# Loading the first units of a fused attention and MLP kernel over three DMA queues, and a new order of loads on a fourth engine's queue

## The chip, the cores and the metric

The kernel runs on one core of a Trainium2 chip. A core has a matrix engine (TensorE, PE; its weight loads are shown apart as PEld), a vector engine (VectorE, DVE), a scalar engine (ScalarE, ACT), GpSimd (POOL) and SyncE (SP), each with its own in-order queue of instructions, and 16 DMA engines that serve all of them. SP and ACT issue transfers over hardware queues; GpSimd issues them over a software queue, whose transfers can also turn fp32 into bf16 on the way. The metric is the device time in microseconds (us), the median of several runs; less is better.

## The reference

A retention layer (attention with decay in place of softmax) feeds a two-layer MLP with exact GELU.

```python
def _attn_ref(q, k, v):                       # each (8, 8, 576, 64) fp32: batch, heads, positions, head size
    scores = scale * np.matmul(q, k.transpose(0, 1, 3, 2))
    gamma = 1.0 - 2.0 ** (-5.0 - np.arange(H, dtype=np.float32))
    rel = pos[:, None] - pos[None, :]
    Dmat = np.where(rel >= 0, gamma[:, None, None] ** rel[None, :, :], 0.0)
    return np.matmul(scores * Dmat[None, :, :, :], v)

x = attn_out.transpose(0, 2, 1, 3).reshape(4608, 512)
h = x @ w_in                                  # (512, 2048)
g = 0.5 * h * (1.0 + erf(h / sqrt(2)))
out = g @ w_out                               # (2048, 512)
```

## The kernel before

**Units.** The 576 positions of each of the 8 batches are cut into chunks of 128 with a tail of 64. A unit is one chunk of one batch (or two tails together); 36 units of 128 rows give the 4608 rows of x. Four units are one block of 512 rows of the MLP. Units 0 to 3 are the first chunks of batches 0 to 3 and need nothing from earlier chunks; they stand alone, later units go in pairs.

**A unit's path.** q and k are turned by PE (`turn`, line 401, into PSUM tile qk_ps, copied by DVE or ACT into qkT), multiplied into scores (`scores`, line 439, tile sc), multiplied on DVE by the decay mask (`masked`, line 488, tile ret, line 507; for first chunks the mask is near, made by ACT at line 164), and multiplied by v on PE (`inner`, line 523, tile o_ps). DVE also makes vh, v scaled by the decay (line 516), from which `state` (line 548, tile u_ps) builds what later chunks need. `evacuate` (line 622) copies o_ps into x; later chunks are multiplied there by dqT (line 636). dqT is extended by four products on GpSimd (line 280), the items dq2, dq3, dq4 and dq0 of the load order. Then follow the first MLP product (`mlp1`, line 652, tile hT, Gelu on ACT into g_all) and the second (`mlp2`, line 683, tile oT, for block 0; a seven-product scheme, `mlp2_fast`, for the others, whose operands wt are four pairs of subtractions of w_out, line 715).

**The planner.** All instructions are put out by a Python loop (line 1110 on) that keeps an estimated time for each engine and chooses PE's next piece of work. It decides with estimated landing times (`land`) and durations; the result is a fixed order on each engine. On the chip the order stays, and semaphores make each instruction wait for its operands. Where nothing is due in the first 16 us, it puts in matmuls on zeros (`warm`, line 1077).

**Loads.** The list ORDER (line 321) is the order of GpSimd's items: wi0 to wi7 and wo0 to wo7 are the eighths of w_in and w_out, q4 the q of unit 4, io the constants, dq a product on dqT. GpSimd keeps up to eight loads in flight: each further one waits for the eighth ahead of it. All loads of units 0 to 3 but two go into the bf16 tile early by this queue. The two are q and k of unit 0: SP and ACT load them as fp32 (line 114), and `either` (line 371) casts them on DVE or ACT, whichever is free first by the planner's count, once `cast_due` (lines 320 and 1049) says that they have landed. A cast is an instruction in that engine's queue, and holds what stands behind it until its load has landed. Line 1146 lets a unit be turned only when its casts are out.

Of the kernel before, what the change touches and what calls it, by code (L numbers as in the profile page):

```python
# [9 lines left out]
FP32 = mybir.dt.float32  # L10
# [7 lines left out]
def kernel(  # L18
# [14 lines left out]
    nc = tc.nc  # L33
    ctx.enter_context(tc.manual_schedule())

    B, H, S, D = q.shape
# [5 lines left out]
    C = 128  # L42
# [28 lines left out]
    N_QKT = 4  # L71
# [4 lines left out]
    ALLOW = 0  # L76
    AHEAD = 14
    RATE = 3.8
    HOT = 7.5
    SLACK, SB, PER_G, PER_B, TURN0 = 1.6, 9.0, 8.0, 40.0, 3.0  # L80
    FINE = 0.38
# [9 lines left out]
    tr_pool = ctx.enter_context(tc.tile_pool(name="tr", bufs=1))  # L91
# [19 lines left out]
    first = {}  # L111
    for nm, src, eng in (("q32", q, nc.sync), ("k32", k, nc.scalar)):
        t = first[nm] = o_pool.tile([128, H, D], FP32, tag="o_sb", name=nm)
        eng.dma_start(t, src[0, :, 0:C, :].rearrange("h s d -> s h d"))
    zeros = ld_pool.tile([128, 512], BF16, tag="v32", bufs=N_V32, name="zeros")
    nc.vector.memset(zeros, 0.0)
    lgh = const.tile([128, H, 1], FP32, name="lgh")
# [34 lines left out]
    def early_slice(n, m):  # L152
        return early[:, n * H * D:(n + m) * H * D]
# [55 lines left out]
            on(engine, dur)  # L209


    sw = [0.0]
    turned = [0.0]
    flying = []
    dq_done = {1}
    land = {}
    loaded = {}
# [11 lines left out]
    def qk_tile(name):  # L229
        return ld_pool.tile([128, 4 * H * D], BF16, tag="qk", bufs=N_LD, name=name)  # L230
# [4 lines left out]
    def tiles_of(i):  # L235
        g = groups[group_of[i]]
        if i not in loaded:
            if i < 4:
                loaded[i] = (early_slice(2 * i, 2).rearrange("p (a h d) -> p a h d", a=2, h=H),
                             early_slice(8 + i, 1).rearrange("p (h d) -> p h d", h=H), None)  # L240
            else:
                n = group_of[i]
                if i != g[0]:
                    qk, kn = loaded[i - 1][0], loaded[i - 1][2]
                elif n not in BY_DVE:
                    qk = qk_tile("qk_ld").rearrange("p (a h j d) -> p a h j d", a=2, h=H, j=2)
                    kn = qk[:, 1]
                else:
                    qk = qk_tile("qkb_ld").rearrange("p (a f) -> p a f", a=2)
                    kn = ld_pool.tile([128, H, 2, D], BF16, tag="kn", bufs=N_KN, name="kn_ld") if len(g) > 1 else None  # L250
                loaded[i] = (qk, None if group_of[i] in BY_DVE else ld_pool.tile([128, H, D], BF16, tag="v", bufs=8, name="v_ld"), kn)
        return loaded[i]
# [12 lines left out]
    def load(what, i):  # L265
# [43 lines left out]
        for jj in (j,) if j is not None else range(2):  # L309
# [3 lines left out]
            else:  # L313
# [2 lines left out]
            land[what, i] = sw_dma(0.88, 0.9) if j is not None else sw_dma(0.68, 0.5)  # L316

    tiles_of(0)
    land["q", 0], land["k", 0] = 4.65, 5.2
    cast_due = {("q", 0): (loaded[0][0][:, 0], first["q32"]), ("k", 0): (loaded[0][0][:, 1], first["k32"])}  # L320
    ORDER = ("wi0 io v0 k1 q1 v1 wi1 q2 k2 v2 wi2 k3 q3 v3 wi3 wi4 wi5 wi6 wi7 wo0 wo1 wo2 wo3 wo4 wo5 wo6 wo7 "
             "q4 k4 q5 k5 v4 v5 dq2 q6 k6 q7 k7 v6 v7 q8 k8 q9 k9 v8 v9 dq3 q10 k10 v10 dq4 q11 k11 q12 k12 n11 n12 dq0").split()

    def next_order():
        item = ORDER.pop(0)
        what = item.rstrip("0123456789")
        load(what, int(item[len(what):] or 0))
# [5 lines left out]
    def reload():  # L333
        if next_load[0] < N_G:
            g = groups[next_load[0]]
            if next_load[0] not in BY_DVE:
                ORDER.extend(f"{what}{i}" for what in "qkv" for i in g)
            else:
                ORDER.extend([f"{what}{i}" for what in "qk" for i in g] + [f"n{i}" for i in g if len(g) > 1])
            next_load[0] += 1  # L340
# [10 lines left out]
    def free_time(n):  # L351
        got = frees(n)
        return free_at[got[-1]] if len(got) == n else 1e9

    def bank(shape, dtype, name):
        b = frees(1)[0]
        held.add(b)
        return b, ps.tile(shape, dtype, tag=b, name=name)

    def release(b, when):  # L360
        held.remove(b)
        free_at[b] = when

    def pe(dur, to="full"):
        if mode[0] != to:
            T["pe"] += 0.11
            mode[0] = to
        T["pe"] += dur * (2.0 if T["pe"] < HOT else 1.0)
        return T["pe"] + DRAIN
# [673 lines left out]
    def fire():  # L1043
        now = T["pe"]
        while ORDER and T["pool"] <= now + 1.5:
            next_order()
# [30 lines left out]
    def warm(n):  # L1077
        b, t = bank([128, 512], FP32, "warm")
        for _ in range(n):
            nc.tensor.matmul(t, lhsT=zeros[:, :128], rhs=zeros, start=True, stop=True)  # L1080
        pe((0.32 if T["pe"] < HOT else 0.2158) * n)
        release(b, T["pe"])
# [22 lines left out]
    for _ in range(N_WARM):  # L1105
        b, t = bank([128, 512], FP32, "warm")
# [3 lines left out]
    while True:  # L1110
# [27 lines left out]
        if nA < N_U:  # L1138
            n = group_of[nA]
            g = groups[n]  # L1140
            if n < nT and nA - nB <= 2 and T["dve"] <= now + SB and g[-1] // 4 <= tM1 + N_XB - 1 and nA + len(g) <= AHEAD + RATE * b1:
                acts.append((max(sg[n]["T"], free_time(2 * len(g))), "S"))
# [53 lines left out]
        gap = min(waits) - now  # L1196
        if now < 16 and gap > (0.6 if now < HOT else 0.2):
            warm(int(gap / 0.6) if now < HOT else max(1, round(gap / 0.23)))
        T["pe"] = max(T["pe"], min(waits))
# [33 lines left out]
```

## Time and profile before

| what | value |
|---|---|
| median of 3 runs | 300.47 us (300.14 to 300.9) |
| profiled execution | 300.81 us, span 298.9 us |
| PE, DVE, POOL, ACT busy | 286.1, 226.7, 152.9, 135.1 us |
| PE: the 15 warm matmuls of line 1080 and 7 of line 1107 | between 1.19 and 14.6 us |
| DMA moved | 34.79 MB, mean 116 GB/s |
| GpSimd's queue, SP's queue, ACT's queue | 17.71, 16.26, 0.26 MB |
| loads of early by GpSimd | 10 of 128 KB, issue to landing 4.9 to 6.1 us |
| w_in, w_out by GpSimd | 8 of 256 KB each, median 7.1 and 9.8 us to landing |

A line of the order of time has the start in us, the time from its first to its last instruction, the engine, the line of the kernel, what is written and read with its shape, the count, and in brackets the idle time of the engine ahead of it with what ended it. A table by stretch has a row for each stretch of time, with each engine's busy time and, at the end, the granted PE clock, the busy share of the 16 DMA engines (transfers overlap, so it can be over 1) and the rate. A DMA queue's line has its packets, megabytes and share of the engines' time.

### The profile page before, as it was taken

What the parts mean: (1) busy time and instruction counts of PE and PEld (TensorE: products, weight loads), DVE (VectorE), ACT (ScalarE), POOL (GpSimd) and SP (SyncE); (2) the same over time, 40 slices, a digit from 0 to 9 for tenths busy, and PEclk for the clock granted to TensorE, in tenths of its full rate; (3) what the DMA queues carried; (4) which work ended last, traced back from release to release, by engine and by line L of the source; (5) the groups of instructions that cost most, each with busy time, mean ns of one, the idle gap of its engine ahead of it and who ended that gap; (6) DMA issues with size and microseconds to landing.
All of it is one profiled execution on the core that took longest, in us unless ns stands there. A gap on an engine that the chain in (4) does not pass through costs nothing.

```text
span 298.9 us, 8793 instructions
## 1 busy us (share of the span) xinstructions
PE 286.1 (96%) x3689; PEld 213.8 (72%) x3718; DVE 226.7 (76%) x432; ACT 135.1 (45%) x262; POOL 152.9 (51%) x232
## 2 busy tenths in 40 slices
PE   7899997999999999999998999999999999999994
PEld 2478555888657656667665666666888888888883
DVE  5762059999999889317969489756998999898751
ACT  7656225744343343542542434433554554546421
POOL 8976797899896899996986842000000000000000
PEclk9999999999999999999999999999999999999998
DMA  9999999999999999999979570201001101111014
GB/s 143 166 186 204 182 187 179 214 163 113 155 141 197 189 201 125 155 162 159 139 126 174 83 188 2 72 2 37 35 2 72 71 2 70 44 28 72 35 55 124
DMA packets 112119, 34.79 MB, mean 116 GB/s; under 512 B 89808, under 2 KB 107728, under 8 KB 112080
## 3 DMA queue, kind: packets, MB, share of 16 engines
q0 software_dynamic: 78048, 17.71, 66.8%
q1 hardware_dynamic: 32992, 16.26, 20.2%
q8 instruction: 29, 0.48, 0.7%
q10 hardware_dynamic: 1040, 0.26, 0.4%
q14 instruction: 10, 0.08, 0.1%
HBM read 42.47 MB, written 9.44 MB: 174 GB/s over the span
## 4 chain that ended last, share of the span: by engine, by line
PE 62%; DMA 16%; POOL 16%; issue 3%; DVE 1%; ACT 0%; POOLq 0%; DVEq 0%; ACTq 0%
PE fa L760 17%; PE hT L656 14%; PE fb L760 13%; PE ha L865 7%; PE hb L865 5%; POOL qkb_ld L298 5%; DMA qkb_ld<-in_q_dram 3%; DMA qk_ld<-in_q_dram 3%; POOL kn_ld L305 3%; DMA kn_ld<-in_k_dram 3%; DMA w_out<-in_moe_w_out_dram 3%; POOL early L315 3%; DMA qk_ld<-in_k_dram 3%; PE sc L462 2%; POOL w_in L270 2%
## 5 line engine op out<-in xcount | busy, mean ns | idle before, releaser
L656 PE MATMUL hT<-x,w_in 128*128 128x512 bf16 (+2 forms) x521 | 92.6, 314 | 3.1 <-DVE x L636 1.0
L656 PEld LDWEIGHTS <-w_in 128*128 128x128 bf16 x544 | 49.1, 98 | 26.1 <-issue 3.2
L661 ACT ACTIVATE g_all<-hT 128x512 bf16<-128x512 f32 x64 | 38.2, 597 | 49.8 <-PE hT L656 47.6
L760 PEld LDWEIGHTS <-g_all 128*128 128x128 bf16 x512 | 49.6, 98 | 11.0 <-issue 0.2
L760 PEld LDWEIGHTS <-s 128*128 128x128 bf16 x384 | 37.4, 98 | 8.9 <-issue 0.2
L746 DVE TENSOR_TENSOR o_sb<-fb,t 128x256 f32<-128x256 f32 x48 | 19.9, 417 | 25.4 <-ACT t L375 12.9
L870 ACT ACTIVATE g_all<-tt 128x512 bf16<-128x512 f32 x36 | 22.6, 630 | 29.4 <-DVE tt L878 29.3
L298 POOL DMA_DIRECT2D qkb_ld<-in_k_dram x56 | 30.9, 587 | 6.5 <-DMA kn_ld<-in_k_dram 4.7
L760 PE MATMUL fa<-w_out,g_all 128*128 128x256 bf16 x256 | 33.1, 273 | 0.0
L305 POOL DMA_DIRECT2D kn_ld<-in_k_dram x44 | 30.4, 731 | 5.2 <-PE u_ps L557 2.3
L298 POOL DMA_DIRECT2D qkb_ld<-in_q_dram x56 | 31.3, 599 | 2.2 <-DMA qkb_ld<-in_k_dram 1.2
L507 DVE TENSOR_TENSOR ret<-sc,mskp 128x512 bf16<-128x512 f32 x44 | 27.2, 677 | 3.2 <-PE sc L462 3.1
L878 DVE TENSOR_TENSOR tt<-hb,tt 128x512 f32<-128x512 f32 x36 | 24.5, 687 | 5.2 <-ACT tt L375 2.9
L664 ACT ACTIVATE g_all<-hT 128x512 bf16<-128x512 f32 (+1 forms) x36 | 19.2, 550 | 14.2 <-PE hT L656 14.1
L375 ACT COPY t<-fa 128x256 f32<-128x256 f32 x35 | 13.0, 371 | 19.6 <-PE fa L760 19.6
L636 DVE TENSOR_TENSOR x<-o_ps,dqT 128x512 bf16<-128x512 f32 (+1 forms) x36 | 20.9, 619 | 0.8 <-PE o_ps L613 0.6
L865 PEld LDWEIGHTS <-ws 128*128 128x128 bf16 x192 | 18.8, 98 | 2.2
L516 POOL TENSOR_TENSOR vh<-v,dvp 128x512 bf16<-128x512 f32 x14 | 15.1, 1134 | 5.2 <-DMA v<-in_v_dram 5.2
L430 DVE STREAM_TRANSPOSE qkT<-qkb_ld 128x512 f32<-128x512 f32 (+1 forms) x28 | 17.4, 637 | 0.0
L760 PE MATMUL fb<-w_out,g_all 128*128 128x256 bf16 x128 | 16.6, 273 | 0.0
L760 PE MATMUL fb<-w_out,s 128*128 128x256 bf16 x128 | 16.4, 273 | 0.1
L760 PE MATMUL fa<-wt,g_all 128*128 128x256 bf16 x128 | 16.4, 273 | 0.0
(123 smaller groups left out, 445.2 us busy)
## 6 DMA issues: line engine op xcount, KB each, us to landing
out_dram<-o_sb SPq DMA_DIRECT2D x31, 256.0 KB, 2.8
v<-in_v_dram SPq DMA_DIRECT2D x50, 128.0 KB, 4.7
qkb_ld<-in_q_dram POOLq DMA_DIRECT2D x44, 64.0 KB, 3.6
qkb_ld<-in_k_dram POOLq DMA_DIRECT2D x44, 64.0 KB, 3.8
kn_ld<-in_k_dram POOLq DMA_DIRECT2D x44, 64.0 KB, 4.5
w_in<-in_moe_w_in_dram POOLq DMA_DIRECT2D x8, 256.0 KB, 7.1
w_out<-in_moe_w_out_dram POOLq DMA_DIRECT2D x8, 256.0 KB, 9.8
out_dram<-o_sb SPq DMA_DIRECT2D x8, 128.0 KB, 2.4
```

The lines of the kernel that those rows point to most:

```text
L298: nc.gpsimd.dma_start(qk[p0:p0 + 32, "qk".index(what), 0:HP * per].rearrange("p (h x) -> p h x", h=HP), {"q": q, "k": k}[what][2 * bp + jj ...
L305: nc.gpsimd.dma_start(kn[64 * e:64 * e + 64, :, j], k[2 * bp + j, :, ci * C + e:ci * C + C:2, :].rearrange("h s d -> s h d"))
L507: nc.vector.tensor_tensor(r, t, by, op=ALU.mult)
L636: nc.vector.tensor_tensor(x[:, :, n * y:n * y + n], o, dqT[:, :, ci * C:ci * C + n], op=ALU.mult)
L656: nc.tensor.matmul(hT[:, m - m0, :], lhsT=w_in[:, cc, m * 128:m * 128 + 128], rhs=x_tiles[t][:, cc, lo:hi], start=(cc == 0), stop=(cc == N ...
L661: nc.scalar.activation(g_all[:, t % 2, :, m0, :], hT.rearrange("p n (a c) -> p (n a) c", a=2), AF.Gelu)
L664: nc.scalar.activation(g_of(t, 2 * lo // TOK)[:, m0:m0 + n, lo_:lo_ + hi - lo], hT, AF.Gelu)
L746: nc.vector.tensor_tensor(dst, src, f[key], op=ALU.add)
L760: nc.tensor.matmul(dst, lhsT=x[:, kk, :], rhs=y[:, kk, :], start=(name in "125" and kk == 0), stop=(kk == HK - 1), skip_group_check=True)
L865: nc.tensor.matmul(dst[:, m, :], lhsT=a[:, cc, c0:c0 + 128], rhs=y[:, cc, :], start=(name in "125" and m == 0 and cc == 0), stop=(cc == HC ...
L870: nc.scalar.activation(g_of(t, part)[:, m0:m0 + 2], src, AF.Gelu)
L878: nc.vector.tensor_tensor(f[key], f["b"][1], f[key], op=ALU.add)
```

## The change

q and k of unit 1 and v of units 0 and 1 are loaded as fp32: q1 and v0 by SP, k1 and v1 by ACT, right behind the two loads that were there. They go into two tiles that borrow buffers of qkT, two loads in each. Four casts bring them into early; the planner is given landing times for them (HW_AT). GpSimd no longer loads these four. Its list is in another order: q2 is first, the weights are mixed with the loads of units 2 and 3 and with each other, and the dq items stand elsewhere. The planner's start of the software queue (sw) is 7.0 instead of 0.

```diff
+    HW_AT = 5.9, 6.4, 6.9, 7.5
...
+    for nm, src, i, eng in (("q1", q, 1, nc.sync), ("k1", k, 1, nc.scalar), ("v0", v, 0, nc.sync), ("v1", v, 1, nc.scalar)):
+        if len(first) % 2 == 0:
+            t = tr_pool.tile([128, 2, H, D], FP32, tag="qkT", bufs=N_QKT, name="first")
+        first[nm] = t[:, len(first) % 2]
+        eng.dma_start(first[nm], src[i, :, 0:C, :].rearrange("h s d -> s h d"))
...
-    sw = [0.0]
+    sw = [7.0]
...
     tiles_of(0)
+    tiles_of(1)
     land["q", 0], land["k", 0] = 4.65, 5.2
-    cast_due = {("q", 0): (loaded[0][0][:, 0], first["q32"]), ("k", 0): (loaded[0][0][:, 1], first["k32"])}
-    ORDER = ("wi0 io v0 k1 q1 v1 wi1 q2 k2 v2 wi2 k3 q3 v3 wi3 wi4 wi5 wi6 wi7 wo0 wo1 wo2 wo3 wo4 wo5 wo6 wo7 "
-             "q4 k4 q5 k5 v4 v5 dq2 q6 k6 q7 k7 v6 v7 q8 k8 q9 k9 v8 v9 dq3 q10 k10 v10 dq4 q11 k11 q12 k12 n11 n12 dq0").split()
+    land["q", 1], land["k", 1], land["v", 0], land["v", 1] = HW_AT
+    cast_due = {("q", 0): (loaded[0][0][:, 0], first["q32"]), ("k", 0): (loaded[0][0][:, 1], first["k32"]),
+                ("q", 1): (loaded[1][0][:, 0], first["q1"]), ("k", 1): (loaded[1][0][:, 1], first["k1"]), ("v", 0): (loaded[0][1], first["v0"]), ("v", 1): (loaded[1][1], first["v1"])}
+    ORDER = ("q2 io wi0 k2 q3 wi2 k3 v3 v2 wi7 wo1 wi5 wo2 wi3 wi1 wi6 wi4 wo6 wo0 wo5 wo3 wo4 q4 wo7 k5 q5 k4 k6 "
+             "v4 dq2 q7 v5 q6 q8 k7 dq3 q9 v7 v6 k9 dq0 k8 v10 v8 v9 dq4 q10 k10 q11 k12 k11 q12 n12 n11").split()
```

As the two programs' instruction lists stand, the work is otherwise the same: PE has 22 matmuls on zeros before and 15 after (the 7 at the start in both), by the planner's choice; all other matmuls are there in both, in another order in the first 110 us and nearly the same one after it. DVE has three casts of the new loads, ACT one; DVE makes two copies of qkT fewer and ACT two more. DVE's order at the start is: cast q0, cast k0, copy of q0's transpose, cast q1, copy of k0's transpose, cast k1, cast v1, copy of q1's transpose, ret of unit 0. The four small steps that make skew (line 190 before), which ACT's dvp and its load of the Gelu table wait for, stand behind u_sb of the first state instead of ahead of the first ret.

## The prediction

> **What bounds the kernel now.** I read the page's busy shares first, then a table of busy time by stretch, then the order of time around each place where PE stands still.
>
> ```profile
> span 298.9 us, 8793 instructions
> ...
> PE 286.1 (96%) x3689; PEld 213.8 (72%) x3718; DVE 226.7 (76%) x432; ACT 135.1 (45%) x262; POOL 152.9 (51%) x232
> ```
>
> TensorE is the bound over the whole: 12.8 us of the span are without a matmul, and some of the busy time is matmuls on zeros. The profiled run is 300.81 us, its span 298.9; the median of the three runs is 300.47. I work with differences and add them to the median.
>
> ```profile
> core 0: us, PE busy (x) PEld busy (x) DVE busy (x) ACT busy (x) POOL busy (x), PEclk, DMA share, GB/s
> 0.00:6.00 6.00, 4.41 (x11) 1.06 (x12) 3.15 (x26) 4.42 (x13) 4.85 (x11) 1.00 0.89 140
> 6.00:9.00 3.00, 2.73 (x22) 1.27 (x20) 2.58 (x9) 2.47 (x6) 3.00 (x5) 1.00 2.36 155
> ...
> 22.00:31.50 9.50, 9.50 (x109) 8.47 (x107) 1.72 (x6) 6.20 (x13) 5.63 (x7) 1.00 1.28 204
> 31.50:39.30 7.80, 7.75 (x39) 3.57 (x38) 0.00 (x0) 1.64 (x4) 6.91 (x8) 1.00 2.05 170
> 39.30:52.00 12.70, 10.92 (x173) 6.85 (x175) 11.32 (x18) 4.72 (x9) 10.92 (x14) 1.00 2.38 187
> 52.00:125.00 73.00, 71.70 (x1139) 51.78 (x1145) 67.53 (x119) 32.55 (x63) 65.85 (x113) 1.00 1.34 164
> ```
>
> The head (to 22 us) is short of data, from 22 to 39 us PE has no gap, from 39 to 52 us it loses 1.8 us while DVE is at 89%, and after 52 us both are nearly full, so what PE is late at 52 us it stays late. The change can act only through two marks: when oT starts (31.55) and what is lost from 39 to 52.
>
> ```profile
> 22.42 0.41 PE L542 MATMUL o_ps<-ret,early 128*64 128x128 bf16 x8
> ...
> 31.55 7.93 PE L689 MATMUL oT<-w_out,g_all 128*128 128x512 bf16 x35
> ...
> 44.77 2.71 DVE L516 TENSOR_TENSOR vh<-v_ld,dv 128x512 bf16<-128x512 bf16 x2
> ...
> 45.83 1.09 POOL L280 TENSOR_TENSOR dqT<-dqT,step 128x512 f32<-128x512 f32 x1
> ...
> 47.54 0.41 PE L542 MATMUL o_ps<-ret,vh 128*64 128x128 bf16 x8 [0.60 <-DVE vh L516]
> ...
> 51.74 1.03 PE L656 MATMUL hT<-x,w_in 128*128 128x256 bf16 x8 [0.81 <-DVE x L636]
> ```
>
> The reader is to see two of PE's largest single waits in the last two lines, and their cause in the third and fourth: two vh products take 2.71 us where one takes 0.68; the second (2.11 us) ends 0.57 us behind GpSimd's multiplication of dqT.
>
> **The change part by part.** *Transfers.* It takes four bf16 loads off GpSimd (issue 0.88 to 1.13 us each) and puts four fp32 loads on SP and ACT. GpSimd's bf16 loads issued at 7.09, 7.96 and 8.83 landed at 12.7, 13.5 and 14.2: 0.8 us of the DMA engines each. With both hardware queues alone (3.0 to 4.0 us: 1108 packets in the microsecond) a 1024-packet fp32 load costs 0.92. So the engines get 4 x 0.12 = 0.5 us more to do, and q2 ahead of wi0 and the weights mixed with w_out change who waits:
>
> - last w_in: 24.3 before, plus 0.5, plus wo1 and wo2 now ahead of it (w_in and w_out land about 1.25 us apart): 27.3. PE comes to it at about 29.5: hidden.
> - last w_out: 34.7 before, plus 0.5, plus q4 ahead (0.8): 36.0. It is needed 28 matmuls of 0.216 behind the start of oT, 38 or later: hidden by 2 us; if oT started 2.5 us earlier, it would be the next thing late.
> - q4 to k5: the last of them 38.7 before, 39.2 now; its use is behind oT, near 40: hidden.
>
> *The landing that decides.* In the program's DVE order the casts stand in the queue as: cast q1, copy of k0's transpose, cast k1, cast **v1**, copy of q1's transpose, and only then ret of unit 0 and all of attention. v1 is last on ACT's queue. ACT in turn holds the cast of v0 ahead of k1's copy. q's packets end about 1 us ahead of its cast at 4.58. Six loads at 0.92 from about 1.8 us end at 7.3, so v1 lands at **8.3** if the hardware queues are served alone. But GpSimd's q2 is under way from about 3.7, as w_in was. How they share, the trace shows at 55 to 62 us:
>
> ```profile
> q0 software_dynamic: 1666, 0.58, 70.6%
> q1 hardware_dynamic: 3805, 1.01, 67.4%
> ```
>
> Equal time for either queue. So from 3.7 three queues get a third each: SP's 1.84 us take 5.5, ACT's last 0.3 take 0.6 more: 9.8, landed **10.7**. I take 10.7, by that row, and keep 8.3 as the lower end.
>
> *DVE from there,* by rows of 5 to 22 us: cast 0.43, copy 0.42, ret pair 1.28, vh 0.68, ret pair 1.28, vh 0.68, ret pair 1.28, u_sb 0.69, the four small skew steps 0.67 (they now stand here), copy 0.42, x 0.69, vh 0.68, ret pair 1.28: 10.5 us without a gap, 10.7 + 10.5 = 21.2. Unit 3's o_ps runs 21.3 to 21.6, 1.1 us ahead of before (22.42). The first ret comes at 11.6 (before: 7.77), but the loads of units 2 and 3 behind it were late anyway.
>
> *PE from there.* Before, 8 groups of w_in at 256 columns (0.87) and 4 at 128 (0.44) were left behind unit 3: 8.7 us, 31.55. In the changed order 10 and 4 are left (fewer ran in the head): 10.5, so 21.6 + 10.5 = 32.1. The activation table for Gelu is loaded behind skew: 18.1 + 0.33 + 1.28 + 0.20 = 19.9 (before: 9.7); six Gelus (4 x 0.38, 2 x 0.60) and the copy of x for unit 3 (0.58) stand in ACT's queue until 23.25, and PE needs that x at 22.9: 0.4 more. oT starts at 32.5, **0.95 late**. The 7 warm matmuls removed (22 to 15, about 0.22 each) sat in waits; they free nothing by themselves. For v1 at 8.3, q3 (landing about 12.6) sets unit 1's product instead; then w_in comes nearer to the path, and the same count gives oT at about 31.1, 0.4 early.
>
> *39 to 52 us.* GpSimd's four dqT products move in its queue. Counting issues (each waits for the eighth load ahead), dq3 falls near 39.5, dq0 from 43.9 to 45.0, both ahead of vh (now 45.7); dq4 (0.62) near 49, on the four wt subtractions. At 52.71 and 61.93 dqT products ran beside ret and x, which read PSUM, and these kept their usual 0.6 to 0.68; so only vh and wt can be hit. I take back the 0.60 wait on vh and nothing of the 0.81 wait on x, since dq4 holds DVE for up to 0.62 ahead of it; ends: 0 and 0.60 + 0.81 = 1.41. The Trainium skill (SBUF — State Buffer, "Who interferes with whom") says that a DVE operation with two SBUF inputs and a GpSimd operation exclude each other for the whole instruction; the 2.11 us product agrees, and by the rule a dqT product that met vh again would give back nothing, net +0.95.
>
> *Casts.* Three on DVE (0.43 to 0.56) and one on ACT (0.58) lie in the head, in the chain above or ahead of v1.
>
> **Sum:** +0.95 − 0.60 = +0.35, 300.47 + 0.35 = **300.8**. This is no change: under 0.3% (0.9 us) a measurement of this kernel (300.14 to 300.9 in three runs) can't tell.
>
> **The rivals.**
>
> *Served first (faster).* v1 lands near 8.3, oT starts 0.4 early, and 0.60 of the waits goes: −1.0, 299.5; with all of the 1.41, 298.7. For it: at 3 to 4 us hardware packets wrote 286 GB/s, against 155 for GpSimd's at 6 to 9 (bf16, read at twice that). Against it: the even shares at 55 to 62.
>
> *The cast of v1 blocks DVE for longer (slower).* The place is the head of DVE's queue; each microsecond of v1 behind 10.7 is a microsecond at oT. It decides from 11.3 on. If queues take turns packet by packet, w_in's packets (twice as long or more) push it: counted over all engines, 1024 turns of 0.9 + 0.9 + 0.8 ns (2.7 us), 512 with w_in's 2.45 (2.2), 512 with k2's (1.3), then ACT's rest (0.6): 10.5, landed 11.4; any delay of v0 on ACT adds. +0.35 + 0.7 = +1.05, 301.5; with nothing given back from 39 to 52, 302.1. For it: in 55 to 62 hardware packets were more numerous than GpSimd's, so turns aren't strictly equal; that speaks half against. The Trainium skill (DMA: Bandwidth & Descriptors, "Queues, rings and completion order") has the engines take turns between queues packet by packet, and under "Issuing engines are not separate DMA queues" says that spreading loads over engines saves only issue time. By these the time is this rival's.
>
> *PE goes cold.* Between 10 and 15 us PE does little (sc, three warm groups, transposes). The first seven warm matmuls took 0.64 us each, the later ones 0.22, so a slower start exists; if it came back, some 1.5 us of matmuls up to 17 us would take twice as long: +1.5 with my sum, 302.3. Against it: no gap in that stretch is over 2 us by my count.
>
> *No effect at all,* as the weights' stream hides it: 300.5, inside my forecast's own range and counted there.
>
> **How the numbers follow.** Forecast 0.38 (own range 300.1 to 301.6), served first 0.25, v1 later 0.28, cold 0.09. Of the forecast's share about 0.29 is within 0.3%, 0.07 slower, 0.02 faster; served first gives 0.23 faster, 0.02 same; v1 later 0.25 slower, 0.03 same; cold 0.08 slower, 0.01 same. Together faster 0.25, same 0.35, slower 0.40. The range 299.0 to 302.4 leaves out the best end of the served-first case and the tails of the slow ones.
>
> **What would show it.** Right: DVE's cast of v1 near 10.7 with an idle stretch ahead; first ret near 11.6; unit 3's o_ps near 21.3; oT near 32.5; a Gelu table load near 18.5; vh pairs of 1.28 at 46, and no 0.60 wait there. Wrong: v1's cast before 9.5 or behind 11.5; oT before 31.5; DVE or PE waits from 52 on that differ by over 1 us from before, which I have put at nothing.

## The result and the profile after

| | before | after |
|---|---|---|
| median, four runs each | 300.34 us (300.14 to 300.9) | 304.28 us (303.97 to 304.45) |
| ratio, 95% interval | | 1.0127 (1.011 to 1.0145) |
| profiled execution, its span | 300.81, 298.9 us | 304.3, 302.1 us |
| first ret on DVE | 7.77 us | 13.44 us |
| start of oT | 31.55 us | 35.80 us |

The changed kernel is slower by 3.94 us; 300.8 had been predicted, no change. The spans differ by 3.2 us, the profiled executions by 3.5, and the rest is that the profiled execution before lay 0.47 above its median. First, from the changed kernel's page, the span and the busy times:

```profile
span 302.1 us, 8817 instructions
...
PE 290.0 (96%) x3711; PEld 215.2 (71%) x3711; DVE 227.1 (75%) x433; ACT 137.0 (45%) x265; POOL 149.2 (49%) x228
```

PE is busy 3.9 us longer with the same work and fewer matmuls on zeros. Some 1.4 us of this are records that the trace before lacks: it has 3689 matmuls for its 3718 weight loads, and behind the start of oT, where the work is the same, it shows 258.1 us busy against 259.5. The other 2.5 us lie ahead of oT, so it isn't waits alone: some matmuls got slower there. The table by stretch of the changed kernel shows where:

```profile
6.00:9.00 3.00, 2.31 (x23) 1.48 (x21) 1.61 (x4) 3.00 (x11) 2.90 (x4) 1.00 1.61 190
9.00:12.00 3.00, 1.98 (x8) 0.71 (x7) 0.00 (x0) 0.82 (x3) 0.85 (x2) 1.00 1.44 179
12.00:16.00 4.00, 2.10 (x21) 1.53 (x22) 3.24 (x7) 1.63 (x5) 2.44 (x4) 1.00 2.06 168
...
39.30:52.00 12.70, 12.70 (x171) 7.39 (x171) 7.07 (x12) 4.52 (x9) 12.70 (x16) 1.00 2.68 172
52.00:125.00 73.00, 72.20 (x1159) 51.44 (x1157) 69.87 (x123) 33.52 (x64) 62.06 (x107) 1.00 1.35 161
```

Between 9 and 12 us DVE does nothing at all, and PE gets through 8 matmuls in 1.98 us of busy time. From 39 to 52 us PE has no gap, where before it lost 1.78 us. DVE's order of time in the changed kernel tells what the head waits for:

```profile
12.76 0.43 DVE L382 CAST early<-first 128x512 bf16<-128x512 f32 x1 [4.34 <-DMA first<-in_v_dram]
13.11 0.42 DVE L382 COPY qkT<-qk_ps 128x512 bf16<-128x512 bf16 x1
13.44 1.28 DVE L516 TENSOR_TENSOR ret<-sc,near 128x512 bf16<-128x512 f32 x2
...
19.17 1.29 DVE L516 TENSOR_TENSOR ret<-sc,near 128x512 bf16<-128x512 f32 x2 [2.06 <-PE sc L456]
...
49.02 1.70 DVE L525 TENSOR_TENSOR vh<-v_ld,dv 128x512 bf16<-128x512 bf16 x2
50.65 1.70 DVE L724 TENSOR_TENSOR wt<-w_out 128x1024 bf16<-128x1024 bf16 x2
...
54.07 1.27 DVE L645 TENSOR_TENSOR x<-o_ps,dqT 128x512 bf16<-128x512 f32 x2
```

The cast of v1 stands at the head of DVE's queue for 4.34 us. And there is a second gap that the prediction does not have: at 19.17 DVE waits 2.06 us for scores of PE. PE's order of time in the changed kernel:

```profile
13.57 0.61 PE L456 MATMUL sc<-qkT 64*128 64x128 bf16 x8 [2.44 <-DVE qkT L382]
...
24.92 0.41 PE L551 MATMUL o_ps<-ret,early 128*64 128x128 bf16 x8
...
35.80 7.93 PE L698 MATMUL oT<-w_out,g_all 128*128 128x512 bf16 x36
...
50.77 0.64 PE L551 MATMUL o_ps<-ret,vh 128*64 128x128 bf16 x16
```

Eight score matmuls take 0.61 us, where before they took 0.40, as this line of the kernel before shows:

```profile
11.47 0.40 PE L447 MATMUL sc<-qkT 64*128 64x128 bf16 x8
```

oT is 4.25 us late; o_ps of units 4 and 5 starts just as late (46.52 before), but runs through without the wait of 0.60 inside it. DVE's instructions from 194 us on, which stand in the same order in both, are 3.22 us late to the end.

### The profile page after: what moved, and what is told of

Its sections match the earlier page's. It is cut to its first block, busy times and chain, and to the rows that moved or that the text cites. A ratio compares the mean times of both kernels' runs of the same rounds, so it can differ in the third digit from the quotient of the medians.

```text
span 302.1 us, 8817 instructions
## 1 busy us (share of the span) xinstructions
PE 290.0 (96%) x3711; PEld 215.2 (71%) x3711; DVE 227.1 (75%) x433; ACT 137.0 (45%) x265; POOL 149.2 (49%) x228
## 4 chain that ended last, share of the span: by engine, by line
PE 81%; DVE 8%; DMA 5%; issue 2%; POOL 2%; ACTq 0%; DVEq 0%; POOLq 0%
PE hT L665 24%; PE fa L769 18%; PE fb L769 13%; PE ha L874 7%; PE hb L874 5%; DMA first<-in_v_dram 4%; PE oT L698 3%; PE sc L471 3%; PE o_ps L551 2%; PE o_ps L622 2%; DVE s L737 2%; PE qk_ps L416 1%; DMA qkb_ld<-in_k_dram 1%; DVE x L645 1%; PE u_ps L566 1%
## 5 line engine op out<-in xcount | busy, mean ns | idle before, releaser
L665 PE MATMUL hT<-x,w_in 128*128 128x512 bf16 (+2 forms) x544 | 93.6, 317 | 0.1
L769 PEld LDWEIGHTS <-s 128*128 128x128 bf16 x384 | 37.0, 98 | 10.7 <-DVE s L737 1.5
L769 PE MATMUL fa<-wt,s 128*128 128x256 bf16 x128 | 16.5, 273 | 0.8 <-DVE s L737 0.8
## 6 DMA issues: line engine op xcount, KB each, us to landing
w_out<-in_moe_w_out_dram POOLq DMA_DIRECT2D x8, 256.0 KB, 10.5
```

The lines of the kernel that those rows point to most:

```text
L665: nc.tensor.matmul(hT[:, m - m0, :], lhsT=w_in[:, cc, m * 128:m * 128 + 128], rhs=x_tiles[t][:, cc, lo:hi], start=(cc == 0), stop=(cc == N ...
L769: nc.tensor.matmul(dst, lhsT=x[:, kk, :], rhs=y[:, kk, :], start=(name in "125" and kk == 0), stop=(kk == HK - 1), skip_group_check=True)
```

## The experiments

Theory A: the casts of the two v loads stand in in-order queues before their data is there, and all of attention waits behind them. Theory B: the new order of GpSimd's list. Theory C: PE runs slow ("cold") in the head because its waits are no longer filled. Theories D and E ask why v1 lands so late. The kernel before was run beside each; its medians there were 300.3 to 300.8 us with runs from 299.1 to 303.6, so the ratios have intervals of 0.24 to 0.5% on either side, and differences under some 0.8 us mean nothing. The line numbers of kernels with inserted lines are shifted.

### 1. The planner is told the measured landings

```diff
-    HW_AT = 5.9, 6.4, 6.9, 7.5
+    HW_AT = 6.9, 8.0, 11.4, 12.7
```

> The changed kernel with one line edited: the landing times that its planner is told for q1, k1, v0 and v1 are the measured ones (6.9, 8.0, 11.4, 12.7 us) and no longer 5.9 to 7.5. The loads themselves stay. The plan then puts both casts of v on ScalarE behind k1's copies, and VectorE makes ret of units 0 to 2 without a cast of v ahead of it. Theory A (the casts of v0 and v1 stand too early in the in-order queues of ScalarE and VectorE, and all of attention waits behind them): first ret near 8.5 instead of 13.44, oT starts 2 to 4 us earlier than 35.80, time 300.3 to 302. Theory B (the new order of GpSimd's list costs the time): oT moves by less than 1 us, time 303.3 or more. Theory C (TensorE runs cold between 8 and 20 us): between them, sc and transposes still 0.6 us, time 302 to 303.

Measured: 302.25 us, 1.0057 (1.0028 to 1.0086). PE's order of time in this kernel, with its first hT:

```profile
16.70 0.40 PE L456 MATMUL sc<-qkT 64*128 64x128 bf16 x8
...
18.12 0.61 PE L665 MATMUL hT<-x,w_in 128*128 128x128 bf16 x8
...
23.55 11.51 PE L665 MATMUL hT<-x,w_in 128*128 128x256 bf16 x104 [0.72 <-ACT x L384]
34.90 2.32 PE L698 MATMUL oT<-w_out,g_all 128*128 128x512 bf16 x9
```

The first ret comes at 8.09, so DVE is no longer blocked, and 2 us of the time come back. But oT gains 0.9 us only. (The profiled execution took 303.69 us, 1.44 over its median, so trace and time do not go closely together here.) The plan, told that v lands late, puts the first o_ps at 17.03, behind transposes, five matmuls on zeros at the slow rate and a group of scores; PE goes through these from 14.00 on without a wait, and the casts of v0 and v1, which ScalarE makes from 13.29 to 14.41, are done long before. hT starts at 18.12, where before it started at 11.80, and all of it piles up behind unit 3. The block on DVE is one part of the loss; hT that starts late on a slow PE is another.

### 2. The old order, with the new loads

The changed kernel with GpSimd's list as before, less the four loads: "wi0 io wi1 q2 k2 v2 wi2 ...".

> The changed kernel with GpSimd's list in the order of the kernel before, less the four loads that SyncE and ScalarE have; the four fp32 loads, their casts and the planned landing times stay as changed, so k1's and v1's casts stand ahead of all ret on VectorE. Theory A (too early casts): first ret again behind v1's landing, 12 us or later, time 302.8 to 304.5. Theory B (the new order costs the time): time 300 to 302. If w_in ahead of q2 takes still more of the DMA engines from v1, v1 lands later than 12.76 and the time may pass 304.3.

Measured: 304.67 us, 1.0152 (1.0102 to 1.0202). v1's cast starts at 13.31, later than 12.76, with two of w_in now ahead of q2. Theory B falls from this side.

### 3. The new order, without the new loads

The kernel before with "wi0 io v0 k1 q1 v1" and behind it the changed order.

> The kernel before with the changed order of GpSimd's list alone: wi0 io v0 k1 q1 v1 stay at its head on GpSimd's queue in bf16, and behind them stands the changed order. Theory A (the casts of the new loads cost the time): within 1 us of before, 299.5 to 301.3. Theory B (the new order costs it, as fewer groups of w_in are there to fill the head): oT later than 31.55 by 2 us or more, time 302 or more.

Measured: 299.59 us, 0.9963 (0.9938 to 0.9989). PE's order of time:

```profile
32.09 7.93 PE L689 MATMUL oT<-w_out,g_all 128*128 128x512 bf16 x35
...
47.20 0.64 PE L542 MATMUL o_ps<-ret,vh 128*64 128x128 bf16 x16
```

and DVE's vh products ahead of that o_ps, no longer beside a product on dqT:

```profile
45.31 1.28 DVE L516 TENSOR_TENSOR vh<-v_ld,dv 128x512 bf16<-128x512 bf16 x2
```

oT is 0.54 later than before, yet the kernel is about 1 us faster: o_ps of units 4 and 5 has no wait inside it and starts 0.34 ahead of where its second half started before. The order is the part of the change that is not at fault, and this kernel has the lowest ratio measured here. The loss belongs to the four loads and to the plan that comes with them: 1.0127 against 0.9963.

### 4. PE's waits filled

The changed kernel with 18 more matmuls on zeros in TensorE's waits; `fill(k)` puts out k of them.

```diff
+    FILL = {(1, 0): 3, 0: 1, (1, 1): 2, (2, 0): 2, 1: 10}
...
     def turn(n, jj, half):
+        if (n, jj) in FILL:
+            fill(FILL[n, jj])
...
     def scores(n):
+        if n in FILL:
+            fill(FILL[n])
```

> The changed kernel with 18 more matmuls on zeros (128x512) on TensorE, put ahead of the transposes and scores that wait for data between 8 and 17 us; order of everything else unchanged. Theory A (the late cast of v1): what waits for v1 waits as before, the landing of v1 stays 12.7; time down by 0.6 us at most, 303.6 to 304.5. Theory C (TensorE is cold until 20 us and its slow matmuls lie on the path behind v1's cast): sc of units 1 and 2 back from 0.6 to 0.4 us, VectorE's wait of 2.06 us for sc at 19.17 gone, oT 1.5 to 2 us earlier, time 302.0 to 302.8.

Measured: 302.01 us, 1.0047 (1.002 to 1.0073): 2.4 us of the loss gone by adding work. Matmuls on zeros by line (17 of the 18 new ones have a record), in ns (least, median, most), first in the changed kernel:

```profile
L1089 PE MATMUL warm<-zeros x8: 391/634/635, 9.6 to 22.2; 128*128 128x512 bf16 x8
```

and in this one:

```profile
L1094 PE MATMUL warm<-zeros x17: 379/379/631, 6.5 to 13.8; 128*128 128x512 bf16 x17
L1100 PE MATMUL warm<-zeros x8: 379/379/389, 11.3 to 19.9; 128*128 128x512 bf16 x8
```

PE's order of time in this kernel:

```profile
16.78 0.40 PE L461 MATMUL sc<-qkT 64*128 64x128 bf16 x8
...
22.63 0.41 PE L556 MATMUL o_ps<-ret,early 128*64 128x128 bf16 x8
...
33.51 3.83 PE L703 MATMUL oT<-w_out,g_all 128*128 128x512 bf16 x16
```

v1's cast starts at 12.65, as in the changed kernel, but scores take 0.40, DVE's wait of 2.06 is 0.20, and unit 3 and oT are 2.29 us earlier. So theory C is shown for 2.3 us of oT's 4.25.

### 5. Measured landings and filled waits together

The landing times of the first experiment, and FILL = {0: 1, (1, 0): 1, 1: 1, (2, 1): 4, (3, 0): 1}.

> The first experiment (measured landing times for the planner) with 8 more matmuls on zeros ahead of the scores and transposes that wait before 14.5 us. If the late casts and the cold TensorE are two causes that add up, the scores take 0.4 us from about 9 us on, oT starts at 32 to 33.5 (34.90 without the matmuls on zeros, 33.51 with these alone) and the time is 300 to 301.3. If both were one cause, oT stays near 33.5 or later and the time near 302.

Measured: 301.86 us, 1.0043 (1.0017 to 1.007). oT starts at 33.80. The two do not add up: this is no better than filling alone, as the expectation had it for a single cause. What the traces show is that PE is fast from about 9.4 us on and that hT still starts late, at 17.07. That this late start keeps oT back is argued and not shown.

### 6. GpSimd's loads start later

The changed kernel, with five products of 128x512 on GpSimd (on a part of dqT that is overwritten later) ahead of q2.

> The changed kernel with five multiplications of 128x512 on GpSimd ahead of its first load, so that all of its loads start some 5 us later and SyncE's and ScalarE's six fp32 loads have the DMA engines to themselves until about 7 us. Nothing else moves. If sharing with GpSimd's queue makes v1 late (theory D), v1's cast starts at 7.5 to 8.5 us (six loads at 0.92 from 1.8 us) and no longer at 12.76. If the two hardware queues are as slow by themselves (theory E), it stays behind 11. The time is not the question: w_in, k2 and q3 come 5 us later, 303 to 308.

One run, 303.05 us. DVE's order of time in this kernel, for v1's cast:

```profile
10.21 0.43 DVE L385 CAST early<-first 128x512 bf16<-128x512 f32 x1 [1.37 <-DMA first<-in_v_dram]
```

The DMA queues of this kernel from 4 to 7 us, SP's and ACT's (packets, MB, share of the 16 engines' time):

```profile
q1 hardware_dynamic: 1422, 0.36, 72.0%
q10 hardware_dynamic: 1242, 0.31, 62.7%
```

of the changed kernel from 9 to 12 us, all three queues:

```profile
q0 software_dynamic: 888, 0.26, 79.1%
q10 hardware_dynamic: 897, 0.23, 52.4%
q1 hardware_dynamic: 200, 0.05, 12.6%
```

and of its last microsecond, 11 to 12:

```profile
q10 hardware_dynamic: 415, 0.11, 80.2%
q0 software_dynamic: 412, 0.05, 79.7%
```

Neither theory alone is right. Left alone, the two hardware queues moved 2664 packets in 3 us: a load of 1024 takes 1.15 us and not 0.92, and v1 lands at 10.2 (GpSimd's packets come in again from about 8.5 us on, so quite alone it would be a little less). Sharing puts another 2.5 us on top. The last two fences show how. From 9 to 12 us ACT's queue and GpSimd's had almost the same number of packets, 897 and 888, but not the same time, 52.4% and 79.1%: they took turns one packet for one, and w_in's larger packets were among GpSimd's. From 11 to 12 us it is 415 against 412. So ACT's queue got 299 packets a microsecond through over the three, and 415 in the last, where the two hardware queues alone got 888.

### 7 and 9. q1 and k1 alone, then with filled waits

Seven: v0 and v1 back on GpSimd behind wi0 ("wi0 io v0 v1 q2 k2 q3 ..."), HW_AT = 6.9, 8.0. Nine: the same with FILL = {0: 1, (1, 0): 1, (2, 0): 3}.

> q1 and k1 alone over SyncE's and ScalarE's queues (landing times 6.9 and 8.0), v0 and v1 back on GpSimd's queue in bf16 behind wi0; the changed order behind that. No cast of v stands on VectorE or ScalarE. If v's fp32 loads and casts cost the time (theory A), first ret near 8.5, oT within 1 us of 32.09 (the changed order with all four on GpSimd) and time 299 to 300.8. If two fp32 loads beside GpSimd's queue cost as much by themselves (theory D in its strong form), GpSimd's q2 and k2 land behind 13.5 and the time is over 301.5.

> q1 and k1 alone over the hardware queues (v0 and v1 on GpSimd's, as in the run of that name, 301.71 us), with 5 more matmuls on zeros ahead of the scores and transposes that wait between 6.7 and 11.6 us. If the cold TensorE is what is left of the loss there (theory C), the scores of units 1 and 2 take 0.4 us instead of 0.61, oT starts 1 to 2 us ahead of 33.50 and the time is 299.6 to 300.7. If the fp32 loads cost by the late landings of GpSimd's own q2 and k2 (theory D), oT gains under 0.5 us and the time stays over 301.3.

Measured: seven 301.71 us, 1.0034 (1.001 to 1.0058); nine 300.09 us, 0.9981 (0.9954 to 1.0008). PE's order of time in seven:

```profile
12.68 0.61 PE L456 MATMUL sc<-qkT 64*128 64x128 bf16 x8
...
33.50 7.93 PE L698 MATMUL oT<-w_out,g_all 128*128 128x512 bf16 x36
```

and in nine:

```profile
12.44 0.40 PE L461 MATMUL sc<-qkT 64*128 64x128 bf16 x8
...
31.50 3.83 PE L703 MATMUL oT<-w_out,g_all 128*128 128x512 bf16 x17
```

Five matmuls on zeros take 2.0 us from oT. The time of seven fell in what theory D had named, but its cause was theory C's. With experiment 4 this makes a table of four, in ratios to the kernel before:

| | waits as planned | waits filled |
|---|---|---|
| q1, k1 and both v over SP and ACT | 1.0127 | 1.0047 |
| q1, k1 alone | 1.0034 | 0.9981 |

The two v loads, with their places in the lists, cost 0.7 to 0.9% in either column, the cold PE 0.5 to 0.8% in either row.

### 8, 11 and 12. Parts of the new order on the kernel before

Eight moves dqT's products alone, eleven all from q4 on, twelve all up to wo7.

> The kernel before with only the four multiplications that make dqT moved in GpSimd's list to where the changed list has them (dq2 behind v4, dq3 behind k7, dq0 behind k9, dq4 behind v9). The head of the list is that of before, so oT stays at 31.5. If the collision of dqT's multiplication with vh is what the changed list takes away, the vh pair takes 1.28 to 1.7 us in place of 2.71, the wait of 0.60 us on vh is gone, and the time is 0.5 to 1.2 us below before. If not, it is within 0.3 us.

> The kernel before with the changed order of GpSimd's list from q4 on alone (loads of units 4 to 12 and dqT's multiplications); the head, all w_in and w_out stand as before. The order alone gave 0.9963; dqT's multiplications alone gave nothing. If the loads of units 4 to 12 in the new order bring it, oT starts at 31.5 as before, the 39 to 52 us stretch loses 1 us less and the time is 299 to 300. If the head's order brings it, the time is within 0.4 us of before.

> The kernel before with the changed order of GpSimd's list up to wo7 alone (q2 and q3 ahead, w_out mixed with w_in, wi1 late, q4 ahead of wo7); from k4 on the list stands as before. The whole changed order on the kernel before gave 0.9963, its tail alone 1.0009, dqT's multiplications alone 1.0001. If the head brings the gain, the ratio is 0.995 to 0.998. If the gain needs head and tail together, it is 0.999 to 1.002.

Measured: 1.0001 (0.9975 to 1.0027), 1.0009 (0.997 to 1.0049) and 1.0001 (0.9978 to 1.0025). None brings the 0.9963 of the whole. In eight, DVE's order of time has

```profile
44.65 2.33 DVE L516 TENSOR_TENSOR vh<-v_ld,dv 128x512 bf16<-128x512 bf16 x2
```

GpSimd's

```profile
44.94 1.28 POOL L280 TENSOR_TENSOR dqT<-dqT,back 128x512 f32<-128x512 f32 x1
```

and PE's

```profile
51.66 1.03 PE L656 MATMUL hT<-x,w_in 128*128 128x256 bf16 x8 [1.06 <-DVE x L636]
```

vh is shorter than the 2.71 of before but meets another of dqT's products, dq0, and the wait on x grows from 0.81 to 1.06. So this run did not take the collision away, and can't tell what it is worth. Whether the gain of experiment 3 needs head and tail together, or is smaller than it looks, stays open.

### 10. The kernel before, not warmed

The 15 matmuls on zeros behind 6 us are taken out of the kernel before.

```diff
         b, t = bank([128, 512], FP32, "warm")
-        for _ in range(n):
-            nc.tensor.matmul(t, lhsT=zeros[:, :128], rhs=zeros, start=True, stop=True)
         pe((0.32 if T["pe"] < HOT else 0.2158) * n)
```

> The kernel before without the matmuls on zeros that its plan puts into TensorE's waits behind 6 us (15 instructions; the 7 at the very start stay). Nothing else moves: loads, order and casts are those of before. Theory C (TensorE stays cold when its waits are not filled): sc, transposes and o_ps take 0.6 us until 17 us or later, oT 1 to 2.5 us later than 31.55, time 301.5 to 303. If the matmuls on zeros are without effect, as the prediction put the seven that the change takes away, the time is within 0.5 us of before.

Measured: 301.15 us beside 300.75, 0.9998 (0.9963 to 1.0034). PE's order of time:

```profile
17.19 0.61 PE L447 MATMUL sc<-qkT 64*128 64x128 bf16 x8
...
32.88 7.93 PE L689 MATMUL oT<-w_out,g_all 128*128 128x512 bf16 x36
```

Here theory C's mechanism came: PE is cold until about 17.8 us and oT 1.33 late. Its price didn't show: a cost of 1.33 us would be 0.44%, outside the interval, though one of 0.3% would lie inside it. The two kernels have the same order, so each DVE instruction can be laid beside its twin: 1.33 us late at 40 us, 0.77 at 52, 1.2 from 62 to 160, and from 176 us on within 0.05. The first 0.56 came back at the vh pair, which was late by 1.33 while dqT's product was not (46.01 us, 45.83 before), and so met less of it:

```profile
46.10 2.16 DVE L516 TENSOR_TENSOR vh<-v_ld,dv 128x512 bf16<-128x512 bf16 x2
```

At 61.11 us another vh met the next product on dqT (1.12 us, 0.68 before), and 0.45 was lost again. The other 1.2 went at one place, which PE's order of time in the kernel before shows and this kernel's doesn't have:

```profile
163.67 0.25 PE L462 MATMUL sc<-qkT 32*128 32x128 bf16 x2 [1.00 <-issue]
```

There PE stood still for 1.00 us in the middle of 32 matmuls that wait for nothing the profile shows. That this is room in the plan, which takes up a late PE, isn't shown. Experiment 8 comes to the same 32 at 163.44 and runs through them, while stops of this kind stand at other places in experiments 4 and 5; one line of each, in this order:

```profile
163.44 0.85 PE L462 MATMUL sc<-qkT 32*128 32x128 bf16 x32
165.03 0.75 PE L476 MATMUL sc<-qkT 32*128 32x128 bf16 x26 [0.69 <-issue]
104.35 0.33 PE L476 MATMUL sc<-qkT 32*128 32x128 bf16 x6 [2.71 <-issue]
```

So the stop may belong to the one profiled execution of the kernel before, and the two spans of 298.9 us may be level by luck. What a delay of PE in the head costs at the end stays open below about 1 us.

## Why the prediction was wrong

**What bounds the kernel, and the two marks: right so far as the traces go.** oT came 4.25 us late, and 39 to 52 us gave back a part. Whether "what PE is late at 52 us it stays late" holds is open. In the changed kernel 1.03 of the 4.25 are back by the end of the span, but the stop of 1.00 us at 163.67 in the trace before is almost as much.

**The landing that decides: right in kind, mis-sized by 2.06 us.** v1's cast does hold DVE's queue, and the first ret stands right behind it, as worked out. It came at 12.76, not 10.7. Two terms were off. The 0.92 us a load was read from a stretch of one microsecond (3.0 to 4.0); over 3 us the two queues alone need 1.15 (experiment 6). With that, v1 alone lands at 10.2, so the lower end of 8.3, and with it the rival "served first", could not be had. And the sharing was taken as equal time, by a row of 55 to 62 us; in the head it was one packet for one, 897 against 888 in 52.4% and 79.1% of the time, as the second rival had it. The Trainium skill (DMA: Bandwidth & Descriptors, "Queues, rings and completion order") says that the engines take turns packet by packet; these counts of the profile's packets agree. That rival's 11.4 was too early as well: it used 0.9 ns a hardware packet, and at the 1.13 of experiment 6 (3 us over 2664) some 4760 hardware packets that it counted from 3.7 us on take 1.1 us more, 12.5.

**DVE's chain: 10.5 us from v1's cast, right only on a warm PE.** In experiment 4 it took 10.0 us from the cast (12.65) to unit 3's o_ps (22.63). In the changed kernel it took 12.2, with 2.06 of it DVE waiting for cold scores. The prediction has 10.6 for the same stretch, so its rows were 0.6 too long. They hid that much of the 2.2 us that the slow PE costs here, and 1.56 is left to see in the sum below.

**PE goes cold: the step that failed.** It stood as a rival with 0.09, argued away because "no gap in that stretch is over 2 us by my count" (the longest was 2.44, and experiment 10 was cold with none over 1.54). And the seven warm matmuls that the plan drops were costed at nothing: "they free nothing by themselves". That is true of their own time, but such matmuls are what makes PE fast in the head: without the fifteen behind 6 us it is slow until 17.8 us (experiment 10), with 18 more in the changed kernel it is fast from about 9.2 us (experiment 4). That the seven alone would have done it, no run shows. In the changed kernel the matmuls up to 20 us took half as long again or more, 0.61 us for 0.40 and 634 ns for 379, and 2.3 us of oT's delay is that. The price given to this rival, 1.5 us, was two thirds of it.

**PE from unit 3 on: right.** 10.5 us of hT predicted, 10.53 measured (25.27 to 35.80); the wait of 0.4 us on x behind the late Gelu table didn't come. Together: 2.06 (v1) + 1.56 (chain) + 0.03 − 0.4 = 3.25, against the 3.30 by which oT missed 32.5; the time missed 300.8 by 3.48.

**39 to 52 us: right at its place, in sign, reason and size.** The 0.60 on vh was taken back because dqT's products move away from it. In the changed kernel DVE is 4.25 us late up to the vh pair and 3.66 behind it (x at 54.07, before at 50.41): the pair takes 1.70 instead of 2.71, and dq4 costs wt 0.42 of that. In experiment 3 the pair takes 1.28, and PE's wait is gone as well. Experiment 8 doesn't speak against it, as dq0 met vh there. That PE has no wait on x either was not foreseen, but other waits of up to 0.83 us came behind 52 us, and how much of the 0.60 is left at the end the traces can't tell.

**Hidden transfers: right so far as PE shows it.** It has no wait on w_in or w_out from 25.27 on.

## What to carry to other kernels

A planner's landing times are part of the kernel: an in-order engine pays for each optimistic one with all that stands behind the waiting instruction, so measure them, in the mix of queues that will run. Matmuls on zeros in a wait are not idle work: before removing any, or before adding a wait, look at how long matmuls of one shape take in that stretch, and price the whole stretch at the slow rate. And before a difference between two traces is called a gain or room in the plan, look for stops that may belong to one execution alone: here one stop of 1.00 us in one trace is most of what makes a delay of 1.2 us look free.

## What the runs showed of the hardware

- PE's speed is not in the granted clock: the column says 1.00 from 9 to 16 us, where sc x8 takes 0.61 us instead of 0.40. Only the durations tell.
- Work without a gap, not the absence of long gaps, made PE fast. In the changed kernel it stayed slow with no gap over 2.44 us, and turned fast at about 19.9, after matmuls without a gap of over 0.3 us from 14.77 on: 5.1 us. Before it took from 1.19 to about 6.6, in experiment 4 from 1.20 to about 9.2, in 10 from 11.76 to about 17.8: 5.4, 8.0 and 6.0 us. And 5.5 us without a gap, 1.19 to 6.71 us in the changed kernel, were not enough: a gap of 0.69 followed, and PE was still slow behind it. The Trainium skill (TensorE: Matmul & The Clock Gate, "What's actually happening") states a window of about 3.4 us that runs by itself and must be met busy; an estimate from that page for gapless work is 3.4 to 6.8 us, by where in the window it starts. Three of the runs lie in its upper half, experiment 4 lies 1.2 us above it, so the estimate doesn't hold here. Of the window itself no run here shows anything.
- PE can stand still inside a group of matmuls that waits for nothing the profile shows, 0.69 to 2.71 us, at another place in each of the traces of before and of experiments 4 and 5. What it waits for is open.
- Issuing on ACT's queue grew dearer with each load: 0.49, 0.73 and 1.52 us, and the first table load on ACT moved from 1.25 to 3.56. It cost nothing visible here.
